# Reordered loads, norms and transposes in the forward and backward pass of a linear-attention block

## The chip, the cores and the metric

The kernel runs on one core of a Trainium2 chip. The time is the device time of one execution in microseconds (us), and the median of several executions stands for a kernel. A core has five engines that run beside each other and each take their instructions strictly in the order in which the program lists them: TensorE (PE, matmuls and transposes by matmul; its weight loads are shown as PEld), VectorE (DVE), ScalarE (ACT), GpSimd (POOL) and SyncE (SP, which here does nothing but issue DMAs). Matmuls write into PSUM, a small memory of a few banks, from which DVE and ACT take the results away. DMA transfers are issued from SP's queue (SPq), or from POOL's, and run on 16 DMA engines that all queues share.

## The reference

The kernel computes one transformer block and its whole gradient. With S = 2048 rows, D = 640 columns, H = 32 heads of 20 columns and F = 1728:

```
phi  = lambda t: where(t > 0, t + 1, exp(t)) + 1e-6
xn   = layernorm(x);  q, k, v = split(xn @ wqkv)
kv   = sum over s of phi(k)^T v        (per head);   z = sum over s of phi(k)
o    = (phi(q) kv) / (phi(q) z + 1e-6)
h    = x + o @ wo
hn   = layernorm(h)
out  = h + (silu(hn @ w1) * (hn @ w3)) @ w2
```

The outputs are `out` and, for a given `grad_out`, the gradients of x, wqkv, wo, w1, w3 and w2. Inputs and outputs are bf16.

## The kernel before

Rows are handled in 16 tiles of 128. The whole order of the work is written out by hand: the program lists the instructions of all engines in one sequence, and each engine takes its own out of it. Nothing is planned by a scheduler. So moving a call in the Python text moves its instructions on the queues of their engines, and only there. Where a tile is ready too late, the engine that wants it stands, and so does everything behind on that engine. A hardware DMA also waits until the eighth one before it has landed, since eight semaphores are used in turn.

The first part (about 0 to 85 us) goes over the row tiles t = 0 to 15 in one loop. Each pass makes K of tile t: five matmuls per half of 320 columns (`p1_half`, line 268) of the turned, normalized x (`pqT`) by the K columns of wqkv, into a PSUM tile `big` that has two buffers. ScalarE takes exp and relu out of it (`phi`, lines 295 and 296, tiles mq and rq), and two DVE instructions, held back by one tile (`held`, lines 299 and 300), make phi(k) of them in `pk_all`. At t = 6, 7, 9 and 11 a Q tile is made in the same way (`q_tile`), in the same PSUM buffers. From t = 7 on, TensorE also works on M = phi(k)^T xn (`m_part`, line 430). kv and v are never formed: M is multiplied by the V columns of wqkv later (`kvT_block`).

Ahead of its use a tile is normalized: DVE makes mean and variance (`stat`), POOL takes the inverse root (`ln_rs`, line 155), and then either DVE normalizes (line 161 and following), or, for the tiles 10, 12 and 14, ScalarE (`norm_act`, line 166), for which POOL also makes the bias `nb` (line 170). From tile 8 on, `p1_norm` then issues the transposing DMA into `pqT` (line 251) on SP. Where in pass t these steps stand is written in the table `v_steps`: "N" and "S" stand before the pass's own exp and relu, in turn with the held DVE instructions (R); "A" stands after the exp and relu and ahead of the Q tile of the pass, "B" behind the Q tile, and "L" after that.

Three tables and lists put DMAs into the passes: `outs` (stores of xn and phi(k) to DRAM, for later), `trickle` (pieces of w1 and w3; `w13` is the list of their loads), and the calls behind the loop. SP issues one DMA after the other, each 0.5 to 3.6 us, and a DMA whose source is not ready holds up all that follow on SP.

After the loop, M is finished row block by row block (`m_end`, which also sends each block through a transposing DMA to `mT`), the four tiles r of normalized phi(q) are made (`r_head` is `r_row`, DVE's work, and then `r_T`, a transposing DMA from SP), and the weights `wo`, `w1`, `w3` and `w2T` come in.

From 76 us on, `f2_wT` makes five blocks of the product of kv and wo, each turned by a DMA from SP into `Wp` (line 709). `f2_half` multiplies the turned r by Wp (lines 655 and 657), adds x, and makes the second layer norm's statistics; `f2_hn` normalizes. `q_out` and `r_store` store phi(q) and r to DRAM from POOL's queue. Then follow the MLP, its backward pass, and the backward pass of the attention.

In the last, at 555 us, `q_parts` leaves five blocks qp (here the tile `tri`), each copied from PSUM by ScalarE and DVE (line 1222 and following) and turned by a DMA from SP into `QT` (line 1226). The list of calls `part(n)` steps through them, with loads of the turned xn between (`load_xnT`, line 1242, each a single transposing DMA of 640 KB). After that come the squares for the gradients of kv and wo (lines 1369, 1388), while `fill(n)` puts half gradients of wqkv (line 1335) between them, and then the loads of phi(k) (`load_pk`, tile pkb), of M (`mN`, from `m_v`), the store of `dwoT_d` and the turned wq (`load_wqT`, line 1299).

The lines that order all this, next to those that the diff shows:

```
            for step in steps:
                if step is not R and step[0] == when:
                    p1_norm(step[1])
            if when == "A" and t in QT:
                q_tile(QT.index(t))
```

Of the kernel before, what the change touches and what calls it, by code (L numbers as in the profile page):

```python
# [9 lines left out]
P = 128  # L10
# [8 lines left out]
S, D, H, F = 2048, 640, 32, 1728  # L19
# [36 lines left out]
def kernel(  # L56
# [19 lines left out]
    V, A, T, G, SY = nc.vector, nc.scalar, nc.tensor, nc.gpsimd, nc.sync  # L76
    dma, dmaT, dmaG = SY.dma_start, SY.dma_start_transpose, G.dma_start

    def rows(ap):
        return ap.rearrange("(t p) d -> p t d", p=P)  # L80
# [50 lines left out]
    class Stats:  # L131
# [13 lines left out]
        def part(self, src, t, j, mid=None):  # L145
            if j == 0:
                self.st[t] = cp.tile([P, 2, 6], F32, name="st6", bufs=4)
            V.bn_stats(out=self.st[t][:, j, :], in_=src[:, t, j * HD:(j + 1) * HD])
            if j == 0:
                return  # L150
            V.bn_aggr(out=self.mv[:, t, :], in_=self.st.pop(t)[:])
            if mid is not None:
                mid()
            V.tensor_scalar(out=self.ve[:, t:t + 1], in0=self.mv[:, t, 1:2], scalar1=EPS_LN, scalar2=None, op0=ALU.add)
            G.tensor_tensor(out=self.rs[:, t:t + 1], in0=self.ve[:, t:t + 1], in1=mhalf[:, 0:1], op=ALU.pow)
# [27 lines left out]
    def load_wq(a, b):  # L183
        dma(out=wqkv[:, :, a * HD:b * HD], in_=wq_v[:, :, a * HD:b * HD])
# [62 lines left out]
    def p1_norm(t):  # L247
        xn = x_sb[:, t, :]
        (ln1.norm_act if on_act(t) else ln1.norm)(xn, xn, t)
        if t >= XT_DMA:  # L250
            dmaT(out=pqT[:, :, t * P:(t + 1) * P], in_=xn)
# [132 lines left out]
    def r_T(t):  # L384
        dmaT(out=pqT[:, :, t * P:(t + 1) * P], in_=pqs[t])
# [47 lines left out]
    def m_end(m, js=(0, 1)):  # L433
        mb = mbs[:, m % 4, :]
        acc = macc[m]
        for j in js:
            A.copy(out=mb[:, j * HD:(j + 1) * HD], in_=acc[j][:, 0:HD])
        if m < 2:
            A.copy(out=Z[:, m:m + 1], in_=acc[1][:, HD:HD + 1])
            z_diag(m)  # L440
        if m < DT - 1:
            dmaT(out=mT[:, :, m * P:(m + 1) * P], in_=mb)
# [13 lines left out]
    def load_w2T(a, b):  # L456
        dmaT(out=w2T[:, :, a:b], in_=B_w2[a:b, :])
# [45 lines left out]
    def load_wo():  # L503
        dma(out=wo[:], in_=A_wo.rearrange("(c p) n -> p c n", p=P))

    trickle = {4: w13[0], 5: lambda: w13[1](0, 1), 6: lambda: w13[1](1, 2), 12: w13[2]}

    R = None
    v_steps = {1: (R, ("N", 4)), 2: (("S", 5), R, ("N", 5)), 3: (("S", 6), R, ("N", 6), ("C", 0)),
               4: (("S", 7), R, ("N", 7), ("S", 8)), 5: (R, ("N", 8), ("S", 9)), 6: (R, ("N", 9), ("S", 10)),  # L510
               7: (("S", 11), R, R, ("A", 10), ("L", 11)), 8: (("S", 12), R, R, ("S", 13)),
               9: (("N", 13), R, ("S", 14), ("B", 12)), 10: (R, R, ("S", 15)), 11: (R, ("A", 14), ("L", 15))}
    V_OPS = {"S": stat, "N": p1_norm, "C": p1_scale}

    def xn_out(g, q):
# [12 lines left out]
    for t in range(ST):  # L528
        first = None
        if t < RAW:  # L530
            first = phi_tiles()
            kh = [ps.tile([P, 512], F32, name="k0", tag="m", bufs=2) for _ in range(2)]

            def act(i, j):
                A.activation(first[i][:, j * HD:(j + 1) * HD], kh[j][:, 0:HD], (AF.Exp, AF.Relu)[i],
                             scale=ln1.rs[:, t:t + 1])

            def between():
                act(0, 0)
                p1_tr(t + 1)  # L540
                act(1, 0)
            k = p1_mm(t, D, between, kh)
            act(0, 1)
            act(1, 1)
        else:
            k = p1_mm(t, D, (lambda: p1_tr(t + 1)) if t + 1 < XT_DMA else None)
        steps = v_steps.get(t, (R,) * len(held))
        for step in steps:
            if step is R:
                held.pop(0)()  # L550
            elif step[0] in V_OPS:
                V_OPS[step[0]](step[1])
        phi(k, pk_all[:, t, :], t, first)
        for when in ("A", "B", "L"):
# [5 lines that stand above are left out]
        if 3 <= t < 7:  # L560
            ghh_chunk(t - 3, lambda: ps.tile([P, 512], F32, name="gp", tag="m", bufs=2))
        m_part(0, M0.get(t, ()))
        if t >= 11:
            V.memset(bd[:, t - 11, :], 0.0)
            make_mask(t - 11)
        if t >= 9:
            m_part(1, [2 * (t - 9), 2 * (t - 9) + 1])
        for f, *n in outs.get(t, ()):
            f(*n)
        if t in trickle:  # L570
            trickle[t]()
# [5 lines left out]
    def r_row(t):  # L577
        r_red(t)
        r_inv(t)
        r_scale(t)  # L580

    def r_head(t):
        r_row(t)
        r_T(t)
# [4 lines left out]
    phi_rest()  # L589
    m_part(1, (14, 15))  # L590
    m_end(1)
    load_wq(4, 6)
    group_out(SC - 1)
    w13[3]()
    z_late((2, 3, 4), big())
    m_part(2, range(10))
    z_rows(((0, 1), (2, 3, 4)), ps.tile([P, 2, 512], F32, name="bigx", tag="big", bufs=2))
# [2 lines left out]
    r_prod(1)  # L600
    m_part(2, range(10, ST))
    m_end(2)
    load_wo()
    for go in w13[4:]:
        go()
    dmaG(out=m_v[:, 0, :], in_=mbs[:, 0, :])
    r_head(0)
    r_prod(2)
    phi_rest()
    m_part(3, range(5))  # L610
    q_tile(6)
    r_head(1)
    r_prod(3)
    phi_rest()
    m_part(3, range(5, 11))
# [4 lines left out]
    phi_rest()  # L620
    m_part(3, range(11, ST))
    m_end(3)
    r_T(2)
    load_w2T(4 * P, 8 * P)
    dmaG(out=m_v[:, 1:4, :], in_=mbs[:, 1:4, :])
    r_head(3)
    r_prod(5)
# [316 lines left out]
    def kv3():  # L944
# [3 lines left out]
    run((q_late, 10, f2_mT), (q_late, 11, kv3), (phi_rest,),  # L948
        (q_late, 12, lambda: (f2_wT(0), f2_wT(1))), (q_late, 13, lambda: (f2_wT(2), f2_wT(3))),
        (f2_wT, 4), (phi_rest,), (q_late, 14), (r_T, 4), (r_head, 5), (r_prod, 7),  # L950
        (q_out, 10, 14), (mlp_ghh, 4),
        (q_late, 15), (w2_room,), (sig_table,), (f2_half, 0, 0), (f2_half, 1, 0), (f2_half, 2, 0), (f2_half, 3, 0), (mlp_ghh, 5),
        (f2_half, 0, 1), (r_store, 4, 5), (f2_half, 1, 1), (f2_hn, 0), (r_store, 5, 6), (f2_half, 2, 1), (f2_hn, 1),
        (f2_half, 3, 1), (f2_m_out,),
        (f2_half, 4, 0, True), (mlp_ghh, 6), (f2_half, 4, 1, True), (f2_half, 5, 0, True), (r_red, 6, (0,)), (f2_hn, 2), (f2_hn, 3),
        (f2_ht, 2), (f2_ht, 3), (load_w2T, 8 * P, 10 * P), (mlp_ghh, 7), (r_red, 6, (1,)), (r_inv, 6), (r_scale, 6),
# [280 lines left out]
    def load_xnT(c):  # L1237

        if c % 2 == 0:
            both = ba.tile([P, 2, DT, W], BF16, name="xnT", tag="ggb", bufs=2)  # L1240
            xnT[c], xnT[c + 1] = both[:, 0], both[:, 1]
        dmaT(out=xnT[c], in_=xn_d[c * W:(c + 1) * W, :])
# [55 lines left out]
    def load_wqT(k):  # L1298
        dmaT(out=wqT[:, k * DT:(k + 1) * DT, :], in_=A_wqkv[:, k * D:(k + 1) * D])
# [12 lines left out]
    load_xnT(1)  # L1312
    part(4)
    part(4)
    load_xnT(2)
    part(20)
    V.reduce_sum(out=gz[:], in_=gz8[:], axis=AX.X)


# [58 lines left out]
        for _ in range(n):  # L1378
            next(jobs, None)

    load_xnT(3)
    load_wqT(0)
    fill(4)
    for m, (a, b) in enumerate(M_H):
        n = (b - a) * DH
# [14 lines left out]
    small = bv.tile([P, ST, D], BF16, name="small", tag="hnN")  # L1400
    mN, gkv_b, gm = (small[:, n:n + DT] for n in (0, DT, 2 * DT))
    gzd = small[:, 3 * DT, :].rearrange("p (m q) -> p m q", q=P)
    dma(out=mN, in_=m_v)
    dma(out=rows(dwoT_d), in_=dwoT[:])

    dx = pool("dx", "right")

    def load_pk(c):
        pkb[c] = dx.tile([P, 2, D], BF16, name="pkb", bufs=4)
        (dma if c < 4 else dmaG)(out=pkb[c][:], in_=pk_v[:, c * 2:(c + 1) * 2, :])  # L1410

    gzb = dx.tile([P, D], F32, name="gzb")
    g_k = gqkv[1] = U1.tile([P, ST, D], BF16, name="g_k", tag="S0")
    for n in range(4):
        load_pk(n)

    for i, (c, ms) in enumerate(SQ_BLOCKS):
        unload(square(wqT[:, 2 * DT:, :], gkvT, i), gm[:, i, :])
# [186 lines left out]
```

## Time and profile before

| | |
|---|---|
| time, median of 3 executions | 819.58 us (819.23 to 820.79) |
| the profiled execution's own time | 820.36 us |
| its span in the trace | 818.6 us (1.76 us lie outside the span) |
| TensorE's clock | 1.00 of full speed |
| TensorE (PE) busy | 811.6 us, 99% of the span |
| DVE, ACT, POOL busy | 55%, 40%, 16% |
| DMA | 162.46 MB, mean 198 GB/s |

How to read the lines that are shown further down. A line of an engine's timeline has the start in us, the duration in us, the engine, the line of the program, the operation, what it writes and reads, the shape, how many instructions were joined in it, and in brackets how long the engine had stood before it and whose end released it. SPq lines are DMAs as SP issues them: the duration is that of the issue, not of the transfer. Matmuls are pipelined and their ends are modelled, so the durations of neighbouring matmul lines overlap, and the start-to-start distance is what counts. The chain that ended last follows the work back from the last instruction, at each step to what released it.

### The profile page before, as it was taken

The numbers are of one execution on the slowest core, as the hardware profiler recorded it, in microseconds if no ns is written. First come the engines' busy times: TensorE is split into PE (matmuls) and PEld (weight loads), VectorE is DVE, ScalarE is ACT, GpSimd is POOL, SyncE is SP. The second block draws the span as 40 slices with busy tenths as digits, with TensorE's granted clock in tenths as the row PEclk, the third lists the DMA queues.
The fourth block names the chain that finished last, engine by engine and source line by source line (L and its number), as shares of the span: only waits on it lengthen the run. The fifth ranks groups of instructions, "written<-read, shape, count | busy, mean of one in ns | idle before, by whom it ended". The sixth has DMA issues, their size and how long they took to land.

```text
span 818.6 us, 13711 instructions
## 1 busy us (share of the span) xinstructions
PE 811.6 (99%) x5261; PEld 501.6 (61%) x5292; DVE 452.7 (55%) x973; ACT 324.8 (40%) x609; POOL 131.7 (16%) x198
## 2 busy tenths in 40 slices
PE   9999999999999999999999999999999999999998
PEld 6777544555555555754577777777777777544444
DVE  7859997998898566300057777772781544200000
ACT  7856688665565666011112212222212334211111
POOL 2243333323222212100001111110220000000000
PEclk9999999999999999999999999999999999999999
DMA  9899899696485556999877877269994888979991
GB/s 262 207 242 277 206 276 302 207 244 174 128 209 158 169 168 168 239 254 243 233 178 181 218 194 193 58 111 181 269 217 93 179 193 153 249 175 235 221 239 37
DMA packets 335889, 162.46 MB, mean 198 GB/s; under 512 B 252560, under 2 KB 329072, under 8 KB 335824
## 3 DMA queue, kind: packets, MB, share of 16 engines
q1 hardware_dynamic: 291920, 120.68, 63.8%
q0 software_dynamic: 7328, 24.48, 8.9%
q10 hardware_dynamic: 36576, 16.42, 8.2%
q8 instruction: 41, 0.67, 0.3%
q14 instruction: 24, 0.20, 0.1%
HBM read 47.09 MB, written 53.43 MB: 123 GB/s over the span
## 4 chain that ended last, share of the span: by engine, by line
PE 96%; DMA 1%; ACT 1%; DVE 1%; issue 0%; SPq 0%; POOL 0%; DVEq 0%
PE mm L395 20%; PE job L1335 19%; PE ghn L1131 14%; PE gxn L1504 8%; PE gw L1086 7%; PE big L268 4%; PE o L913 4%; PE o L859 3%; PE gwo L1219 3%; PE macc L430 3%; PE gr L1188 3%; PE dkv L1441 3%; PE at L657 2%; DMA wqkv<-in_A_wqkv_dram 1%; PE dkv L1369 1%; DMA tri<-tri 1%
## 5 line engine op out<-in xcount | busy, mean ns | idle before, releaser
L1335 PE MATMUL job<-gb,hnN 128*128 128x496 bf16 (+3 forms) x576 | 116.8, 366 | 0.0
L1131 PEld LDWEIGHTS <-ggb 128*128 128x128 bf16 x864 | 84.5, 98 | 33.0
L395 PE MATMUL mm<-pqT,w 128*128 128x512 bf16 x396 | 93.2, 379 | 0.5
L1335 PEld LDWEIGHTS <-hnN 128*128 128x128 bf16 x576 | 55.8, 98 | 61.0
L395 PEld LDWEIGHTS <-w 128*128 128x128 bf16 x540 | 52.6, 98 | 62.9 <-issue 0.6
L1339 ACT CAST obs<-job 128x496 bf16<-128x496 f32 (+4 forms) x56 | 28.5, 510 | 123.6 <-PE job L1335 123.6
L1131 PE MATMUL ghn<-w13a,ggb 128*128 128x320 bf16 x448 | 63.5, 299 | 0.0
L1146 DVE SCALAR_TENSOR_TENSOR wb<-gs,hnb 128x640 f32<-128x640 bf16 x16 | 13.2, 825 | 88.1 <-ACT gs L1143 88.1
L1131 PE MATMUL ghn<-w13b,ggb 128*128 128x320 bf16 x416 | 61.4, 299 | 0.0
L395 PE MATMUL mm<-g2T,w2T 128*128 128x512 bf16 x228 | 58.8, 379 | 0.6
L1086 PE MATMUL gw<-hb,g 128*128 128x512 bf16 (+2 forms) x316 | 58.4, 345 | 0.2
L1086 PEld LDWEIGHTS <-g 128*128 128x128 bf16 x320 | 31.3, 98 | 27.0
L420 ACT CAST ghh<-mm 128x512 bf16<-128x512 f32 x48 | 28.2, 588 | 48.2 <-PE mm L395 41.4
L1196 POOL TENSOR_TENSOR sz<-Zb,g_h 128x640 f32<-128x640 bf16 x16 | 20.2, 1262 | 163.7 <-DVE g_h L1197 163.7
L796 ACT ACTIVATE sig<-mm 128x512 bf16<-128x512 f32 x56 | 33.7, 602 | 25.0 <-PE mm L395 21.6
L1143 ACT ACTIVATE gs<-ghn 128x640 bf16<-128x640 f32 x16 | 11.3, 705 | 76.0 <-PE ghn L1131 76.0
L395 PEld LDWEIGHTS <-w2T 128*128 128x128 bf16 x260 | 25.4, 98 | 23.4
L268 PEld LDWEIGHTS <-pqT 128*128 128x128 bf16 x320 | 30.7, 98 | 13.5 <-ACT pqT L260 0.9
L268 PE MATMUL big<-wqkv,pqT 128*128 128x320 bf16 x250 | 38.4, 299 | 0.2
L1335 PEld LDWEIGHTS <-g 128*128 128x128 bf16 x320 | 31.0, 98 | 11.5
L832 DVE TENSOR_TENSOR gate<-gate,sig 128x1024 bf16<-128x1024 bf16 x28 | 19.3, 689 | 33.9 <-ACT gate L807 31.1
L1091 ACT CAST gw2o<-gw 128x512 bf16<-128x512 f32 (+2 forms) x20 | 10.4, 519 | 66.6 <-PE gw L1086 25.3
(217 smaller groups left out, 1391.2 us busy)
## 6 DMA issues: line engine op xcount, KB each, us to landing
hh_d<-hhT SPq DMA_DIRECT2D x24, 256.0 KB, 2.8
gg_d<-gate POOLq DMA_DIRECT2D x24, 256.0 KB, 4.4
gg_d<-ghh POOLq DMA_DIRECT2D x24, 256.0 KB, 4.1
ggb<-gg_d SPq DMA_DIRECT2D x6, 896.0 KB, 5.3
ggb<-gg_d ACTq DMA_DIRECT2D x6, 832.0 KB, 5.7
ggb<-gg_d SPq DMA_DIRECT2D x2, 1728.0 KB, 13.9
pk_d<-pk_all SPq DMA_DIRECT2D x4, 640.0 KB, 5.4
g<-in_grad_out_dram SPq DMA_DIRECT2D x4, 640.0 KB, 5.7
```

The lines of the kernel that those rows point to most:

```text
L268: T.matmul(acc, lhsT=pqT[:, c, t * P:(t + 1) * P], rhs=wqkv[:, c, n0:n0 + HD], start=(c == 0), stop=(c == DT - 1))
L395: T.matmul(acc[:], lhsT=w[:, c, fc * P:(fc + 1) * P], rhs=rhs[:, c, :], start=(c == 0), stop=(c == DT - 1))
L420: A.copy(out=ghh[n // 2][:, n % 2, :], in_=acc[:])
L430: T.matmul(macc[m][j][:, 0:n], lhsT=pk_all[:, t, m * P:(m + 1) * P], rhs=x_ext[:, t, j * HD:j * HD + n], start=(t == 0), stop=(t == ST - 1))
L796: A.activation(sig[:, i, :], gp[:], AF.Sigmoid)
L859: T.matmul(accs[i, j][:, 0:HD], lhsT=hhT[c][:, fc, i * P:(i + 1) * P], rhs=w2[:, fc, j * HD:(j + 1) * HD], start=(first and fc == 0), stop ...
L913: T.matmul(o2["ps"][:, 0:HD], lhsT=hhT[c][:, fc, i * P:(i + 1) * P], rhs=w2[:, fc, j * HD:(j + 1) * HD], start=(fc == 0), stop=(fc == FT - 1))
L1086: T.matmul(acc[:, 0:fw], lhsT=g2[:, t, m * P:(m + 1) * P], rhs=hb[b][:, t, 0:fw], start=(t == 0), stop=(t == ST - 1))
L1131: T.matmul(acc[:, j, 0:HD], lhsT=ggb[t // 2][:, k, lo:lo + P], rhs=rhs[:, j * HD:(j + 1) * HD], start=(k == 0), stop=(k == NG - 1))
L1335: T.matmul(acc[:, 0:n], lhsT=lhs[:, t, m * P:(m + 1) * P], rhs=rhs(t), start=(t == 0), stop=(t == ST - 1))
L1339: A.copy(out=ob, in_=acc[:, 0:n])
L1504: T.matmul(acc[:, j, 0:HD], lhsT=g, rhs=wqT[:, k, j * HD:(j + 1) * HD], start=(k == 0), stop=(k == 14))
```

## The change

The diff changes the order of calls only; the computation, the number of instructions and the tiles remain. TensorE's and DVE's instructions keep their order. In parts:

1. In the loop, the table `trickle` gets the second load of w1 at t = 7 (before: t = 12), the V columns of wqkv at t = 9 (before: after `m_end(1)`) and the second load of w3 at t = 13 (before: after the last `group_out`). `wo` and the rest of w1 and w3 are loaded after that last `group_out` (before: after `m_end(2)`), and w2T's columns 512 to 1023 after `m_end(2)` (before: after `r_T(2)`).
2. A new step "F" calls `p1_norm` ahead of the exp and relu of the pass. Tile 12's norm on ScalarE stands there at t = 9 (before: "B", behind the exp and relu of K tile 9 and Q tile 2), and tile 14's at t = 11 (before: "A", behind the exp and relu of K tile 11). The transposing DMA of tile 12 moves with it, ahead of that of tile 13.
3. `r_T(1)` goes from the row work of r tile 1 to after `m_end(3)`.
4. The two `r_store` calls of r tiles 4 and 5 stand before and after `q_out`, instead of among the first `f2_half` steps.
5. `load_xnT(2)` comes behind the last `part` step instead of ahead of it, so behind the last transposing DMA of tri.
6. The loads of pkb 0 and 1 come ahead of those of mN and the store of dwoT_d; `load_xnT(3)` and `load_wqT(0)`, which stood ahead of the squares, come behind the loads of pkb 2 and 3.

```diff
--- before.py
+++ after.py
@@ -503,13 +503,13 @@
     def load_wo():
         dma(out=wo[:], in_=A_wo.rearrange("(c p) n -> p c n", p=P))
 
-    trickle = {4: w13[0], 5: lambda: w13[1](0, 1), 6: lambda: w13[1](1, 2), 12: w13[2]}
+    trickle = {4: w13[0], 5: lambda: w13[1](0, 1), 6: lambda: w13[1](1, 2), 7: w13[2], 9: lambda: load_wq(4, 6), 13: w13[3]}
 
     R = None
     v_steps = {1: (R, ("N", 4)), 2: (("S", 5), R, ("N", 5)), 3: (("S", 6), R, ("N", 6), ("C", 0)),
                4: (("S", 7), R, ("N", 7), ("S", 8)), 5: (R, ("N", 8), ("S", 9)), 6: (R, ("N", 9), ("S", 10)),
                7: (("S", 11), R, R, ("A", 10), ("L", 11)), 8: (("S", 12), R, R, ("S", 13)),
-               9: (("N", 13), R, ("S", 14), ("B", 12)), 10: (R, R, ("S", 15)), 11: (R, ("A", 14), ("L", 15))}
+               9: (("F", 12), ("N", 13), R, ("S", 14)), 10: (R, R, ("S", 15)), 11: (("F", 14), R, ("L", 15))}
     V_OPS = {"S": stat, "N": p1_norm, "C": p1_scale}
 
     def xn_out(g, q):
@@ -548,6 +548,8 @@
         for step in steps:
             if step is R:
                 held.pop(0)()
+            elif step[0] == "F":
+                p1_norm(step[1])
             elif step[0] in V_OPS:
                 V_OPS[step[0]](step[1])
         phi(k, pk_all[:, t, :], t, first)
@@ -589,9 +591,10 @@
     phi_rest()
     m_part(1, (14, 15))
     m_end(1)
-    load_wq(4, 6)
     group_out(SC - 1)
-    w13[3]()
+    load_wo()
+    for go in w13[4:]:
+        go()
     z_late((2, 3, 4), big())
     m_part(2, range(10))
     z_rows(((0, 1), (2, 3, 4)), ps.tile([P, 2, 512], F32, name="bigx", tag="big", bufs=2))
@@ -600,16 +603,14 @@
     r_prod(1)
     m_part(2, range(10, ST))
     m_end(2)
-    load_wo()
-    for go in w13[4:]:
-        go()
+    load_w2T(4 * P, 8 * P)
     dmaG(out=m_v[:, 0, :], in_=mbs[:, 0, :])
     r_head(0)
     r_prod(2)
     phi_rest()
     m_part(3, range(5))
     q_tile(6)
-    r_head(1)
+    r_row(1)
     r_prod(3)
     phi_rest()
     m_part(3, range(5, 11))
@@ -620,8 +621,8 @@
     phi_rest()
     m_part(3, range(11, ST))
     m_end(3)
+    r_T(1)
     r_T(2)
-    load_w2T(4 * P, 8 * P)
     dmaG(out=m_v[:, 1:4, :], in_=mbs[:, 1:4, :])
     r_head(3)
     r_prod(5)
@@ -948,9 +949,9 @@
     run((q_late, 10, f2_mT), (q_late, 11, kv3), (phi_rest,),
         (q_late, 12, lambda: (f2_wT(0), f2_wT(1))), (q_late, 13, lambda: (f2_wT(2), f2_wT(3))),
         (f2_wT, 4), (phi_rest,), (q_late, 14), (r_T, 4), (r_head, 5), (r_prod, 7),
-        (q_out, 10, 14), (mlp_ghh, 4),
+        (r_store, 4, 5), (q_out, 10, 14), (r_store, 5, 6), (mlp_ghh, 4),
         (q_late, 15), (w2_room,), (sig_table,), (f2_half, 0, 0), (f2_half, 1, 0), (f2_half, 2, 0), (f2_half, 3, 0), (mlp_ghh, 5),
-        (f2_half, 0, 1), (r_store, 4, 5), (f2_half, 1, 1), (f2_hn, 0), (r_store, 5, 6), (f2_half, 2, 1), (f2_hn, 1),
+        (f2_half, 0, 1), (f2_half, 1, 1), (f2_hn, 0), (f2_half, 2, 1), (f2_hn, 1),
         (f2_half, 3, 1), (f2_m_out,),
         (f2_half, 4, 0, True), (mlp_ghh, 6), (f2_half, 4, 1, True), (f2_half, 5, 0, True), (r_red, 6, (0,)), (f2_hn, 2), (f2_hn, 3),
         (f2_ht, 2), (f2_ht, 3), (load_w2T, 8 * P, 10 * P), (mlp_ghh, 7), (r_red, 6, (1,)), (r_inv, 6), (r_scale, 6),
@@ -1312,8 +1313,8 @@
     load_xnT(1)
     part(4)
     part(4)
+    part(20)
     load_xnT(2)
-    part(20)
     V.reduce_sum(out=gz[:], in_=gz8[:], axis=AX.X)
 
 
@@ -1378,8 +1379,6 @@
         for _ in range(n):
             next(jobs, None)
 
-    load_xnT(3)
-    load_wqT(0)
     fill(4)
     for m, (a, b) in enumerate(M_H):
         n = (b - a) * DH
@@ -1400,9 +1399,6 @@
     small = bv.tile([P, ST, D], BF16, name="small", tag="hnN")
     mN, gkv_b, gm = (small[:, n:n + DT] for n in (0, DT, 2 * DT))
     gzd = small[:, 3 * DT, :].rearrange("p (m q) -> p m q", q=P)
-    dma(out=mN, in_=m_v)
-    dma(out=rows(dwoT_d), in_=dwoT[:])
-
     dx = pool("dx", "right")
 
     def load_pk(c):
@@ -1411,8 +1407,14 @@
 
     gzb = dx.tile([P, D], F32, name="gzb")
     g_k = gqkv[1] = U1.tile([P, ST, D], BF16, name="g_k", tag="S0")
-    for n in range(4):
-        load_pk(n)
+    load_pk(0)
+    load_pk(1)
+    dma(out=mN, in_=m_v)
+    dma(out=rows(dwoT_d), in_=dwoT[:])
+    load_pk(2)
+    load_pk(3)
+    load_xnT(3)
+    load_wqT(0)
 
     for i, (c, ms) in enumerate(SQ_BLOCKS):
         unload(square(wqT[:, 2 * DT:, :], gkvT, i), gm[:, i, :])
```

## The prediction

> **What bounds the kernel now.** I read the page's shares first, then the chain that ended last, then TensorE's timeline in each stretch that the diff touches, and last the queues feeding it there. The page (part 1, part 2's clock row, part 4):
>
> ```profile
> span 818.6 us, 13711 instructions
> PE 811.6 (99%) x5261; PEld 501.6 (61%) x5292; DVE 452.7 (55%) x973; ACT 324.8 (40%) x609; POOL 131.7 (16%) x198
> ...
> PEclk9999999999999999999999999999999999999999
> ...
> PE 96%; DMA 1%; ACT 1%; DVE 1%; issue 0%; SPq 0%; POOL 0%; DVEq 0%
> ```
>
> TensorE (PE) is busy for 99% of the span, at full clock, and 96% of the last chain is its own work. The diff removes no matmul, so it can only win places where TensorE waits, and lose by making new ones. Both are found on TensorE's timeline, where a gap stands in brackets:
>
> ```profile
> 39.98 1.52 PE L268 MATMUL big<-wqkv,pqT 128*128 128x320 bf16 x10
> ...
> 44.33 1.52 PE L268 MATMUL big<-wqkv,pqT 128*128 128x320 bf16 x10
> ...
> 85.57 2.88 PE L657 MATMUL at<-Wp,pqT 128*128 128x320 bf16 x20 [0.24 <-DVE rden L378]
> ...
> 566.50 0.78 PE L1388 MATMUL gkvT<-tri,woT 128*128 128x140 bf16 x10 [0.47 <-DMA tri<-tri]
> ```
>
> Between 24 and 85 us no line has a bracket: in the stretch where most of the diff lies, nothing is there to win. The two gaps shown are the only ones that the diff can close. Ends of matmuls are modelled, so I take start to start: consecutive 128x320 matmuls follow at 0.136 us, and by that measure the first gap costs 0.40 us and the second 0.63. A third, 0.25 us at 96.13 (the turned hn(3), late on DVE), keeps its cause. The measurement can't tell changes under about 0.2% (1.64 us) from none; so even both gaps together (1.03 us) lie below that.
>
> **ScalarE's norms, ahead of exp.** ScalarE (ACT) takes its instructions in order. Its timeline and POOL's:
>
> ```profile
> 32.40 0.70 ACT L295 ACTIVATE mq<-big 128x640 bf16<-128x640 f32 x1 [0.76 <-DVE pk_all L300]
> 33.00 0.70 ACT L296 ACTIVATE rq<-big 128x640 bf16<-128x640 f32 x1
> ...
> 34.84 0.92 ACT L166 ACTIVATE x_sb<-x_sb,nb,ln_rs 128x640 bf16<-128x640 bf16 x1
> ...
> 38.49 0.70 ACT L295 ACTIVATE mq<-big 128x640 bf16<-128x640 f32 x1 [0.76 <-DVE pk_all L300]
> 39.09 0.70 ACT L296 ACTIVATE rq<-big 128x640 bf16<-128x640 f32 x1
> 39.67 0.92 ACT L166 ACTIVATE x_sb<-x_sb,nb,ln_rs 128x640 bf16<-128x640 bf16 x1
> ```
>
> ```profile
> 32.21 0.41 POOL L170 TENSOR_SCALAR nb<-ln_mv,ln_rs 128x1 f32<-128x1 f32 x1
> ...
> 38.30 0.46 POOL L170 TENSOR_SCALAR nb<-ln_mv,ln_rs 128x1 f32<-128x1 f32 x1
> ```
>
> The norm needs nb, and POOL has nb(12) at 32.62 and nb(14) at 38.76, both after the exp that it now precedes could have run (32.40, 38.49). So norm 12 runs from about 32.66, the exp of tile 9 follows 0.81 later (39.67 to 40.48 is the same pair) at 33.47, and its relu ends at 34.76 instead of 33.70. K tile 10's first matmul, 34.44 before, writes the PSUM buffer that this relu releases (two buffers, in the order k9, q2, k10). Before, it started 0.74 after the relu's end, so that it did not wait; a matmul that waits starts about 0.06 after its releaser (566.45 to 566.50 at the tri gap). It now starts near 34.82: +0.38. Likewise norm 14 from 38.80, exp of tile 11 at 39.61 instead of 38.49, relu's end 40.90 instead of 39.79, and K tile 12, due at 39.98 + 0.38 = 40.36, starts near 40.96: +0.60. Together **+0.98 us**. Behind the norms queue only these exps and relus and those of the Q tile after each; the DVE adds that follow have gaps. DVE from 57 to 80 us has none, but it starts from TensorE's Z sums, so it moves along and gives nothing back. Bounds: 0 (if the exps catch up) and 1.11 (if tile 12 keeps the 0.19 that lay between the relu's end and its start).
>
> What the move buys is pqT(12) earlier: it landed at 39.43 for a need at 39.98. TensorE did not wait there, so that is worth nothing.
>
> **Bulk loads.** The w1 load (864 KB) goes from t = 12 to t = 7, behind xn_d; the V columns of wqkv (800 KB) go from after the loop to t = 9; w3 (832 KB) to t = 13; wo and the rest to about 55 us. All are due much later (77 us and after), and no byte is added. Each issue costs SP 0.5 to 1.2 us (its timeline has 1.12 for the w1 load); SP has idle time at these places. The price is in what is queued behind: the turned pqT(12), then pqT(14). In the trace the stretch from 43.2 (pk_d, xn_d, w1, pk_d: 2784 KB) has all landed at 55.45, some 265 GB/s with a starting delay near 1 us. xn_d and w1 together (1540 kB, from 33.0) are then through at 38.8; a turned tile issued behind a w3 part landed 0.7 after it (pqT(9)) and one 2.2 after it (pqT(10)); so pqT(12) lands at 39.5 to 41.0 against a need of 40.4 to 40.96. pk_d and V (1475 kB from 37.9) are through at 43.5, and pqT(14) lands at 44.2 to 45.7 against a need of 44.33 + 0.98 = 45.3. I take **0**, since three quarters of both spans lie ahead of the need; the bound above is 0.4 from these rows and 2 from lower rates (below). A gain is excluded, as no wait is here. At 52 to 75 us the turned mT(2) is issued earlier than before (it landed at 66.50 for 68.34), so nothing is late there.
>
> **The turned Wp blocks, 85 us.** SP's timeline:
>
> ```profile
> 77.38 1.40 SPq L187 DMA_DIRECT2D x_sb<-in_A_x_dram  x1
> 79.66 6.59 SPq L709 DMA_TRANSPOSE Wp<-pkx  x5
> ```
>
> The 0.24 gap is put down to DVE's rden, which was long done; the trace has Wp block 2 issued at 82.39 to 83.60 and landed at 85.48, and the matmuls start at 85.57. x_sb's 960 KB land at 83.44, among the blocks. Since r_T(1) and w2T now precede, SP is free sooner and the x_sb load goes at the end of its release, about 0.8 earlier. Blocks 3 and 4, behind no other load, landed 1.45 and 1.39 after their issue ended; block 2 would land at about 85.0 against 85.17. So **-0.40**; bounds -0.40 and 0 (if the issue time of 1.3 us a block is what counts). w2T's 512 columns, moved ahead of the turned r tiles on SP, and r_T(1), two places later, are needed from 82.7 and 85.6; their cover is over 10 us each.
>
> **tri and xnT(2), 560 us.** SP's timeline:
>
> ```profile
> 554.86 3.87 SPq L1226 DMA_TRANSPOSE tri<-tri  x3
> 558.77 3.34 SPq L1242 DMA_TRANSPOSE xnT<-xn_d  x1
> 562.21 1.22 SPq L1226 DMA_TRANSPOSE tri<-tri  x1
> ```
>
> The last tri block's copy by ACT ended at 561.5, but its transpose waited behind xnT(2)'s issue until 562.21 and landed at 566.45. With xnT(2) behind it, it issues from 561.5 and, with the 2.7 us median to landing, lands near 564.2, ahead of 565.86, when TensorE wants it; even the 4.25 us that it took here would do. **-0.63**, bounds -0.63 and 0 (d, below). Next late are the dkv buffers, with about 0.04 us to spare, so no more than that is taken away again. xnT(2) then lands near 568 (due about 596). xnT(3) and wqT(0), moved behind pk and dwoT_d, land near 580 and 584 (due 604 and 625); mN and dwoT_d may make SP idle for 3 us, as they wait for dwoT's squares; the pkT transposes end about 4 us later, with 5 us to spare. Cost 0; if that cover is gone, up to 1.
>
> **r_store.** Two POOL issues of 0.58 us move ahead of the ln_rs of rows 1 to 3. ve reaches POOL for those before DVE wants them: **0**; bound +0.5, the 96.13 gap growing by one issue.
>
> **Sum.** +0.98 + 0 - 0.40 - 0.63 + 0 = -0.05 us on the profiled execution's 820.36 (818.6 of span and 1.76 outside), 820.31. That execution is 0.78 above the median of the runs shown (819.58); taking it off, **819.5 us**: no difference.
>
> **Rivals.**
> (a) The norms ahead cost nothing: the 0.74 us of room absorbs it, as it would if nb came earlier. Then -1.03, 818.55. For it: nb(12) is only 0.2 later than the old exp; against: 0.81 + 0.2 exceed 0.74, and tile 12 had only 0.19. Still under 0.2%.
> (b) The other side: the bulk loads hold up the turned x tiles. It replaces the 0.98, as a late pqT covers ScalarE's delay. At the 209 GB/s that the window from 24 to 60 us has as its mean, 1475 kB from 37.9 are through at 45.0 and pqT(14) lands 1.4 later, 46.4: +2.07 against 44.33, net +1.0, 820.6. It decides when pqT(14) lands after 47.0 (2.67 late, to cover the 1.03 and 1.64), which takes a rate under 192 GB/s; with 165 it lands at 48.2, net +2.9, 822.5. For it: pqT(10), behind a w3 part, took 4.2 us, and the DMA row is at 9 tenths here. Against: most of that share is transposes, and xn_d and pk_d there landed 655 kB in 3.5 us, starting delay included.
> (c) Wp stays late: +0.35, 819.9, for SP's issue of 1.3 us a block.
> (d) tri lands no earlier, since xnT(1) and POOL's stores are in flight: 820.1.
>
> On (b): the Trainium skill, "DMA: Bandwidth & Descriptors", section "Queues, rings and completion order", says that each DMA engine consumes descriptors in the order of the ring, which for one issuing engine is one ring. By that rule a small transpose does not pass a bulk load of the same queue, and the place chosen for the loads can only cost. The trace agrees as far as it goes: pk_d, issued 1.2 us behind the w1 load, landed 1.66 behind it. By the rule alone, without a rate, the time is that of (b).
>
> **How the numbers follow.** Forecast (sum, with (c) and (d) as its variants) 0.50, (a) 0.17, (b) 0.28, of it two thirds past its point of decision or joined by another loss, something unforeseen 0.05. Slower by over 0.2%: 0.2 from (b), 0.04 from the unforeseen and 0.02 from the forecast's upper bounds, 0.26. Faster: only if more is to be won than the gaps on the timeline, 0.09. Within: 0.65. The range goes from 818.2, (a) with the r rows' gap as well, to 822.0, short of (b) at 165 GB/s.
>
> **What would show it.** In the changed kernel: brackets at K tiles 10 and 12 of 0.3 to 0.6 us, released by ACT's rq; no bracket at the L1388 and L657 groups; pqT(14) landed by 45.3. The prediction is wrong if a bracket with a pqT landing stands at 40 or 45 us, if gaps come at 580 to 625 us (xnT, pkT), or if the time leaves 819.6 by more than 1.64 us.

## The result, and the profile after

The changed kernel took 821.43 us (median of 10 executions) against 819.55 us for the kernel before (10 executions): a ratio of 1.0025, 95% interval 1.0015 to 1.0034. The medians lie 1.88 us apart, and the interval leaves out "no difference". The forecast was 819.5 us, no difference. The time itself lies inside the stated range of 818.2 to 822.0; that the kernel became slower does not fit the forecast.

The page of the changed kernel's profiled execution (821.89 us; span, busy shares, chain that ended last):

```profile
span 820.2 us, 13745 instructions
PE 812.9 (99%) x5292; PEld 501.2 (61%) x5292; DVE 452.7 (55%) x973; ACT 325.4 (40%) x609; POOL 131.4 (16%) x198
...
PE 93%; DVE 3%; DMA 2%; SPq 1%; issue 0%; ACT 0%; POOL 0%; DVEq 0%; ACTq 0%
```

The busy shares hardly differ from before (the 31 matmuls more are records that the first trace of before lacks; the second has 5292 too). The chain tells more: TensorE's part fell from 96% to 93%, and DVE, DMA and SP's queue came in. TensorE's timeline of the changed kernel has new brackets at four places (idle us, then who ended it):

```profile
35.11 1.52 PE L268 MATMUL big<-wqkv,pqT 128*128 128x320 bf16 x10 [0.61 <-ACT rq L296]
...
41.20 1.52 PE L268 MATMUL big<-wqkv,pqT 128*128 128x320 bf16 x10 [0.22 <-ACT rq L296]
...
45.98 1.53 PE L268 MATMUL big<-wqkv,pqT 128*128 128x320 bf16 x10 [0.26 <-DMA pqT<-x_sb]
...
94.90 0.85 PE L658 MATMUL at<-Wp,pqT 128*128 128x320 bf16 x5 [0.86 <-DMA pqT<-pql]
```

The first two are K tiles 10 and 12, waiting for ScalarE's relu; the third is K tile 14, waiting for its turned x; the fourth is the turned r tile 4. The brackets at 85 and 566 us are gone, as forecast. But the kernel before, profiled once more (819.31 us), has neither of them, with nothing changed. TensorE's timeline of that second profile:

```profile
85.11 2.88 PE L657 MATMUL at<-Wp,pqT 128*128 128x320 bf16 x20
...
564.46 1.73 PE L1388 MATMUL gkvT<-tri,woT 128*128 128x140 bf16 x25
```

The 25 gkvT matmuls now run as one group, where the first profile had 15, a wait, and 10. So I use this second profile as the base below. Both traces hold 5292 weight loads, in the same order. The difference of the starts of the same weight load in two traces, followed along the run, is a ladder: it rises by a step where one execution loses time. Against the second profile of before, the changed kernel's ladder is:

| where | step, us |
|---|---|
| the first 10 us | +0.13 |
| K tile 10, ScalarE's relu | +0.77 |
| K tile 12, ScalarE's relu | +0.38 |
| K tile 14, turned x | +0.43 |
| r tile 4, turned r | +1.03 |
| hn(3) and the MLP's first matmuls, net | -0.14 |
| everything after 100 us | 0.0 |
| sum (820.17 - 817.57) | +2.60 |

So 1.58 us come from the K loop, about 0.9 from r tile 4 and what follows it, and nothing from the parts behind 100 us. The medians differ by less than 2.60, since the second profile of before lies 0.24 below that kernel's median and the changed kernel's profile 0.46 above its own.

### The profile page after: what moved, and what is told of

Read it like the earlier page. It is cut to its first block, busy times and chain, and to the rows that moved or that the text cites. A ratio compares the mean times of both kernels' runs of the same rounds, so it can differ in the third digit from the quotient of the medians.

```text
span 820.2 us, 13745 instructions
## 1 busy us (share of the span) xinstructions
PE 812.9 (99%) x5292; PEld 501.2 (61%) x5292; DVE 452.7 (55%) x973; ACT 325.4 (40%) x609; POOL 131.4 (16%) x198
## 4 chain that ended last, share of the span: by engine, by line
PE 93%; DVE 3%; DMA 2%; SPq 1%; issue 0%; ACT 0%; POOL 0%; DVEq 0%; ACTq 0%
PE mm L395 20%; PE job L1336 20%; PE ghn L1132 14%; PE gxn L1506 8%; PE gw L1087 7%; PE o L914 4%; PE o L860 3%; PE gwo L1220 3%; PE gr L1189 3%; PE dkv L1443 3%; PE at L658 2%; PE macc L430 2%; PE big L268 1%; PE mm L268 1%; DVE st L148 1%; DMA pqT<-pql 1%
```

## The experiments

Times are ratios to the kernel before in the same session; their intervals are about +-0.1% (0.8 us), so single steps are read from the ladder, which is one execution of each kernel. Most kernels below are the kernel before with one part of the diff ("alone"), or the changed kernel with one part undone. The new places of w2T's columns and of `r_T(1)` were not run alone.

**Each part alone.** The norms:

```diff
-               9: (("N", 13), R, ("S", 14), ("B", 12)), 10: (R, R, ("S", 15)), 11: (R, ("A", 14), ("L", 15))}
+               9: (("F", 12), ("N", 13), R, ("S", 14)), 10: (R, R, ("S", 15)), 11: (("F", 14), R, ("L", 15))}
...
+            elif step[0] == "F":
+                p1_norm(step[1])
```

> The kernel before with only the norms of tiles 12 and 14 ahead of exp. Theory (each edit pays its own step of the difference of the two traces): K tile 10 waits about 0.8 us and K tile 12 about 0.4 us for ScalarE's relu, +1.15 us, about 820.7 against 819.55. Rival (ScalarE is late only because SP's transfers around it are late): no gap at these tiles, 819.5.

Measured 1.0015 (1.0006 to 1.0024). The ladder has +0.60 at K tile 10 and +0.30 at K tile 12, together 0.89, with all bulk loads in their old places. TensorE's timeline of this kernel:

```profile
34.85 1.52 PE L268 MATMUL big<-wqkv,pqT 128*128 128x320 bf16 x10 [0.43 <-ACT rq L296]
```

So the norms cost by themselves, for the reason that the prediction gave. ScalarE's timeline of the changed kernel shows it:

```profile
32.96 0.92 ACT L166 ACTIVATE x_sb<-x_sb,nb,ln_rs 128x640 bf16<-128x640 bf16 x1 [1.01 <-POOL nb L170]
33.79 0.68 ACT L295 ACTIVATE mq<-big 128x640 bf16<-128x640 f32 x1
34.37 0.69 ACT L296 ACTIVATE rq<-big 128x640 bf16<-128x640 f32 x1
...
39.05 0.92 ACT L166 ACTIVATE x_sb<-x_sb,nb,ln_rs 128x640 bf16<-128x640 bf16 x1 [0.69 <-POOL nb L170]
```

ScalarE stands 1.01 and 0.69 us for POOL's nb, with the exp of a finished K tile behind it in its queue. The relu ends at 35.06, and the waiting matmuls start at 35.11. The rival, no gap without the bulk loads, falls.

The bulk loads (w1, V and w3 into the loop, wo and the rest of w1 and w3 up from after `m_end(2)`):

```diff
-    trickle = {4: w13[0], 5: lambda: w13[1](0, 1), 6: lambda: w13[1](1, 2), 12: w13[2]}
+    trickle = {4: w13[0], 5: lambda: w13[1](0, 1), 6: lambda: w13[1](1, 2), 7: w13[2], 9: lambda: load_wq(4, 6), 13: w13[3]}
...
-    load_wq(4, 6)
     group_out(SC - 1)
-    w13[3]()
+    load_wo()
+    for go in w13[4:]:
+        go()
...
-    load_wo()
-    for go in w13[4:]:
-        go()
```

> The kernel before with only the bulk loads moved (w1, V columns and w3 into the loop, wo and the rest to after the last group_out). Theory (steps add up): only tile 14's turned x is late, by about 0.4 us, 820.0. Rival (bulk loads hold up whatever is turned behind them, and the norms ahead of exp cover a part of that): tile 12, now issued at 36.8 behind xn_d and w1, lands near 41.5 for a need at 40.0, tile 14 near 46.4 for 44.4; +1.9 us, 821.4.

Measured 1.0025 (1.0015 to 1.0035). Tile 12 landed at 39.96 and cost 0.1 at most; tile 14 landed at 45.84 and cost a step of 1.5 us on TensorE's timeline:

```profile
45.88 1.53 PE L268 MATMUL big<-wqkv,pqT 128*128 128x320 bf16 x10 [1.33 <-DMA pqT<-x_sb]
```

The rival had it right: the loads cost 1.5 us alone, not the 0.4 that they add to the norms. Its detail for tile 12 (41.5) was a miss here.

The r stores:

```diff
-        (q_out, 10, 14), (mlp_ghh, 4),
+        (r_store, 4, 5), (q_out, 10, 14), (r_store, 5, 6), (mlp_ghh, 4),
...
-        (f2_half, 0, 1), (r_store, 4, 5), (f2_half, 1, 1), (f2_hn, 0), (r_store, 5, 6), (f2_half, 2, 1), (f2_hn, 1),
+        (f2_half, 0, 1), (f2_half, 1, 1), (f2_hn, 0), (f2_half, 2, 1), (f2_hn, 1),
```

> The kernel before with only the r stores of tiles 4 and 5 around q_out. Theory: POOL's first r store waits for r tile 4 and pushes the 640 KB store of q into the time of the turned r tile 4, which lands over 3 us later: gap of about 1 us at r tile 4, the 0.25 us gap at hn(3) smaller, +0.8 us, 820.4. Rival (the gap at r tile 4 comes from TensorE and Wp being shifted, not from the stores): 819.5, no gap there.

Measured 1.0013 (1.0004 to 1.0022). The gap appears at r tile 4 although nothing ahead of the stores was moved and TensorE did not wait for Wp; the ladder has +1.18 there and +1.13 in all. TensorE's timeline:

```profile
93.40 0.85 PE L657 MATMUL at<-Wp,pqT 128*128 128x320 bf16 x5 [1.00 <-DMA pqT<-pql]
```

The last tri block's transpose ahead of xnT(2), with the transfers behind it (parts 5 and 6 of the diff):

```diff
+    part(20)
     load_xnT(2)
-    part(20)
...
-    load_xnT(3)
-    load_wqT(0)
     fill(4)
...
-    dma(out=mN, in_=m_v)
-    dma(out=rows(dwoT_d), in_=dwoT[:])
...
-    for n in range(4):
-        load_pk(n)
+    load_pk(0)
+    load_pk(1)
+    dma(out=mN, in_=m_v)
+    dma(out=rows(dwoT_d), in_=dwoT[:])
+    load_pk(2)
+    load_pk(3)
+    load_xnT(3)
+    load_wqT(0)
```

> The kernel before with only xnT(2) behind the last turned tri block and the pk, mN and dwoT_d transfers ahead of xnT(3) and wqT(0). Theory: the 0.63 us gap at 566 us goes and nothing comes in its place, 818.9. Rival (the later xnT(3), wqT(0) and pkT transfers give it back, or the time at 566 us is won again by waits behind it): 819.5 or more, with gaps between 575 and 630 us.

Measured 0.9998 (0.9990 to 1.0007): no difference. No gap at 566 us, none between 575 and 630, and also no gain, which the theory had put at 0.63. The gap was not in the usual execution of before. With the old order of these transfers, nine other executions were profiled (the second one of before and eight of kernels with this part untouched); a step at this place is in one of them, of 0.5 us. The theory's mechanism, SP's issue of xnT(2) ahead of the last block, is only a part of it. In the second profile SP was through with xnT(2) at 560.59 and issued the last block at 561.03, when its copies were done, so the order cost nothing. In the two executions with the gap (the first profile of before and the one just named) the block was issued 0.5 to 0.7 us late behind xnT(2), and it also landed 3.0 us after the end of its issue, where the second profile has 1.4. What made that transfer slow stays open.

**One part undone.** The changed kernel with the first diff of these, the norms, reversed:

> The changed kernel with the norms of tiles 12 and 14 back in their old places. Theory (tile 14's turned x lands near 45.9 behind the V columns whatever ScalarE does, so the larger of the two waits counts, not their sum): no gap at K tiles 10 and 12, one of 1.3 to 1.6 us at tile 14; about 821.4, no difference from the changed kernel's 821.43. Rival (steps add up): 1.15 less, 820.3.

Measured 1.0024 (1.0012 to 1.0037), as the changed kernel. Its TensorE timeline has the waits at other tiles, for the DMA now:

```profile
42.15 1.53 PE L268 MATMUL big<-wqkv,pqT 128*128 128x320 bf16 x10 [0.84 <-DMA pqT<-x_sb]
...
47.88 1.53 PE L268 MATMUL big<-wqkv,pqT 128*128 128x320 bf16 x10 [1.20 <-DMA pqT<-x_sb]
```

Steps of 1.0 at tile 12 and 1.4 at tile 14, and no wait for relu at tile 10 (this execution had lost 1.0 us before the first moved load was issued). So undoing the norms wins nothing: they cost about 1.1 us for ScalarE, and they bring tile 12's transpose forward, which the loads ahead of it would otherwise make late. It was expected that tile 12 has no gap; that was a miss.

The r stores' diff reversed:

> The changed kernel with the r stores of tiles 4 and 5 back in their old places. Theory: the gap of 1 us at r tile 4 goes, about 1.0 less, 820.4. Rival (the freed turned Wp blocks bring TensorE there before its operand anyway): 821.4 with a gap at r tile 4.

Measured 1.0017 (1.0003 to 1.0031). The gap at r tile 4 is gone, the ladder is +0.77, +0.38, +0.29 at tiles 10, 12 and 14, with 0.18 at tile 9 ahead of them, and ends at 1.60, 1.0 below the changed kernel's. The ratio agrees within its interval, and could not have told it alone.

V's load back behind the loop:

```diff
-    trickle = {4: w13[0], 5: lambda: w13[1](0, 1), 6: lambda: w13[1](1, 2), 7: w13[2], 9: lambda: load_wq(4, 6), 13: w13[3]}
+    trickle = {4: w13[0], 5: lambda: w13[1](0, 1), 6: lambda: w13[1](1, 2), 7: w13[2], 13: w13[3]}
...
     m_end(1)
+    load_wq(4, 6)
     group_out(SC - 1)
```

> The changed kernel with the V columns' load back behind the loop; w1 stays at t = 7 and the norms stay ahead of exp. Theory (V is the load that holds up tile 14): tile 14 lands near 43.5 and does not wait, the gaps at tiles 10 and 12 (about 1.1 us together) stay, about 0.4 less, 821.0. Rival (the w1 load ahead of it is enough): the gap at tile 14 stays, 821.4.

Measured 1.0011 (1.0000 to 1.0022). Tile 14 landed at 43.23 and did not wait, as expected. But a wait came at another place, for the turned third block of M:

```profile
70.10 0.48 PE L449 MATMUL bigx<-mT,wqkv 128*128 128x140 bf16 x5 [0.62 <-DMA mT<-hx]
```

V's 800 KB and then wo, w1 and w3 now all stand on SP ahead of mT(2), which landed at 70.05 (66.04 in the second profile of before) for a need near 69.2. Here r tile 4 had no gap, with the r stores as in the changed kernel: SP issued its transpose at 87.71, just ahead of the q store's 88.00, and it landed at 92.17, ahead of that store (92.85).

All three back at once (the last diff, and those of the norms and the r stores reversed):

> The changed kernel without the three parts that cost: V's load, the two norms and the two r stores back in their old places; the other moves stay. Theory (the 0.40 us gap at 85 us and the 0.63 us gap at 566 us of the first profile are not in most executions): 819.4, no difference from before. Rival (both are there as a rule, and these moves take them away): 818.5.

Measured 1.0027 (1.0003 to 1.0051), neither of the two expected results. TensorE's timeline shows what was left in:

```profile
40.62 1.53 PE L268 MATMUL big<-wqkv,pqT 128*128 128x320 bf16 x10 [0.59 <-DMA pqT<-x_sb]
69.55 0.48 PE L449 MATMUL bigx<-mT,wqkv 128*128 128x140 bf16 x5 [0.39 <-DMA mT<-hx]
...
609.57 1.52 PE L1444 MATMUL dkv<-small,xnT 128*128 128x320 bf16 x10 [0.55 <-DVE gp L1447]
...
628.27 0.85 PE L1507 MATMUL gxn<-wqT,bd 128*128 128x320 bf16 x5 [1.29 <-DMA bd<-g_k]
```

The w1 load at t = 7, without the norms ahead, makes tile 12 late (0.76 on the ladder); V, wo, w1 and w3, issued from 55 us on ahead of mT(2), make it late (0.57). The last two lie in the stretch that the prediction named for gaps at xnT and pkT, but wait for other transfers. At 610 us DVE had stood 0.92 us for a load of phi(k) that landed at 607.67. At 628 us it is the turned block bd, which SP issued at 624.39, after the pkT transposes that kept it busy until 621.85. Neither the changed kernel's profile nor the tri part's own has these waits. Of the seven profiles with xnT(2) behind the last tri block, two have a wait between 580 and 630 us (the other is the last kernel of this section); of the ten with the old order none has.

**The cost of one load, by place and by queue.** V alone to t = 9, in the kernel before:

```diff
-    trickle = {4: w13[0], 5: lambda: w13[1](0, 1), 6: lambda: w13[1](1, 2), 12: w13[2]}
+    trickle = {4: w13[0], 5: lambda: w13[1](0, 1), 6: lambda: w13[1](1, 2), 12: w13[2], 9: lambda: load_wq(4, 6)}
...
     m_end(1)
-    load_wq(4, 6)
```

> The kernel before with only the V columns' load moved, to t = 9 on SP. Theory (this load alone holds up tile 14): its turned x lands near 45.8, gap near 1.5 us at K tile 14, 821.2. Rival (it takes the w1 load at t = 7 too): landed by 44.4, no gap, 819.6.

Measured 1.0021 (1.0011 to 1.0030). V landed at 44.59 and tile 14's x at 45.31, a step of 1.09 us: most of the 1.5 of all the loads. The same from POOL's queue:

```diff
-    def load_wq(a, b):
+    def load_wq(a, b, q=dma):
-        dma(out=wqkv[:, :, a * HD:b * HD], in_=wq_v[:, :, a * HD:b * HD])
+        q(out=wqkv[:, :, a * HD:b * HD], in_=wq_v[:, :, a * HD:b * HD])
...
-    trickle = {4: w13[0], 5: lambda: w13[1](0, 1), 6: lambda: w13[1](1, 2), 12: w13[2], 9: lambda: load_wq(4, 6)}
+    trickle = {4: w13[0], 5: lambda: w13[1](0, 1), 6: lambda: w13[1](1, 2), 12: w13[2], 9: lambda: load_wq(4, 6, dmaG)}
```

> The same single move, but the V columns are loaded from POOL's queue. Theory of the queue's order (the turned tile waits because it stands behind the load on SP's queue): it lands by 44.4, no gap, 819.6. Theory of the shared engines (the load's bytes take the DMA engines' time from whichever queue): lands near 45.8 again, gap of over 1 us, 821.2.

Measured 1.0035 (1.0022 to 1.0048). POOL issued the load at 41.08, SP the transpose at 43.00, so nothing bulky was ahead of it on its own queue but the pk store of both kernels. V landed at 47.83 and the turned x at 48.48 (45.4 and 46.1 without the 2.4 us that this execution had lost before). So a place behind the load on SP's queue is not needed for the delay; the load's bytes on the shared DMA engines do it from POOL's queue too. The trace's single packets show it: V's run from 43.75 to 47.43, and SP's queue starts none between 43.69 and 46.83, although the issue of the transpose had ended at 44.20. TensorE's timelines, V from SP and then from POOL:

```profile
45.35 1.53 PE L268 MATMUL big<-wqkv,pqT 128*128 128x320 bf16 x10 [0.91 <-DMA pqT<-x_sb]
```

```profile
20.68 0.45 PE L258 MATMUL tr<-ident,x_sb 128*128 128x128 bf16 x5 [1.30 <-DVE x_sb L161]
...
48.53 1.53 PE L268 MATMUL big<-wqkv,pqT 128*128 128x320 bf16 x10 [1.68 <-DMA pqT<-x_sb]
```

(The wait at 20.68 stands before any changed instruction and belongs to this execution, not to the change: an x load landed at 18.09, against 15.39 in the second profile of before. The step at tile 14 is 1.85 against 1.09 from SP, since V, issued at the same point of the loop, landed 0.8 us later; why was not tried.) In both, the turned tile landed 0.7 behind the load. The Trainium skill, "DMA: Bandwidth & Descriptors", section "Issuing engines are not separate DMA queues", says that DMAs of all issuing engines run on the same 16 DMA engines and that another issuing engine saves issue time only; this run agrees. The order on SP's own queue, by which the prediction argued, is too narrow to explain it.

V behind tile 15's transpose, at the end of t = 11:

```diff
-    trickle = {4: w13[0], 5: lambda: w13[1](0, 1), 6: lambda: w13[1](1, 2), 12: w13[2], 9: lambda: load_wq(4, 6)}
+    trickle = {4: w13[0], 5: lambda: w13[1](0, 1), 6: lambda: w13[1](1, 2), 12: w13[2], 11: lambda: load_wq(4, 6)}
```

> The kernel before with only the V columns' load moved, to the end of pass t = 11, behind tile 15's turned x instead of ahead of tile 14's. Theory (it is the place ahead of tile 14 that costs, not the load inside the loop): no gap at K tiles 12 to 15, 819.5. Rival (the load's bytes cost wherever they lie in the loop): the gap moves to the next landing, the store's or mT's readers at 52 to 69 us, 820.5 or more.

Measured 1.0000 (0.9991 to 1.0009), with no step at K tiles 12 to 15. It is the place that costs. The profiled execution has the wait for Wp at 85 us, which is in others too (below).

w1 alone to t = 7, in the kernel before:

```diff
-    trickle = {4: w13[0], 5: lambda: w13[1](0, 1), 6: lambda: w13[1](1, 2), 12: w13[2]}
+    trickle = {4: w13[0], 5: lambda: w13[1](0, 1), 6: lambda: w13[1](1, 2), 7: w13[2]}
```

> The kernel before with only the w1 load moved, to t = 7. Theory (a turned tile waits for whatever was issued ahead of it): tile 12, issued at 36.8 behind it, lands 0 to 0.8 late, tile 14 in time; 819.5 to 820.3. Rival (w1 has 4 us less queued ahead of it there and is through by 38.2): no gap at all, 819.5.

Measured 1.0012 (1.0000 to 1.0025). Tile 12 landed at 40.72, a step of 0.55; tile 14 in time. The step is within the theory's 0 to 0.8; the median, 820.56, is a little above its 820.3.

**The q store first,** then both r stores:

```diff
-        (r_store, 4, 5), (q_out, 10, 14), (r_store, 5, 6), (mlp_ghh, 4),
+        (q_out, 10, 14), (r_store, 4, 6), (mlp_ghh, 4),
```

> The kernel before with the r stores of tiles 4 and 5 directly behind the q store, not around it. Theory (the first r store waits for r tile 4 on POOL and pushes the q store's 640 KB into the turned tile's time): the q store leaves at its old time near 85.6, the turned r tile 4 lands near 91 for a need at 92.5, no gap, 819.6. Rival (it is the r stores' own 320 KB beside it): gap of about 1 us at r tile 4 as with the stores around it, 820.8.

Measured 1.0008 (0.9997 to 1.0019). The step at r tile 4 fell from 1.18 to 0.17; a net 0.5 came at the turned hn soon after. The q store landed at 91.96, the r stores at 93.14 and 93.94, the turned r tile 4 behind all three at 94.20. Without the 1.9 us that this execution had lost before, the q store landed at its old time (90.0; 90.10 in the second profile of before) and the turned tile at 92.3, 1.4 us later than there (90.85). With the stores around the q store (the r stores alone, above) it landed at 93.35, 2.4 us later than there on the ladder. TensorE wants it 1.2 us after 90.85, so the first lateness costs 0.2 and the second 1.2. Both theories hold a part: the r stores' bytes are 1.4 us of the lateness, the push of the q store 1.0. The push is not a wait for r tile 4, as the theory had it (see the r stores, below).

**The kernel before, profiled once more:**

> The kernel before, unchanged, profiled once more. Theory (the gaps of 0.40 us at 85 us and 0.63 us at 566 us are accidents of the first profiled execution, whose time lay 0.8 above the median): at least one of them is missing, span near 817.6. Rival (they belong to the kernel): both are there again at these sizes.

819.31 us, span 817.6, neither gap. Of the sum's -1.03 nothing is left against this execution.

**The best guess for a better version** has V's load at t = 11, as above, and of the tri part only the move of xnT(2) behind `part(20)`:

> The version left over as the best guess: V's load at the end of t = 11 and only xnT(2) moved behind the last turned tri block. Theory (neither gap of the first profile is there as a rule): 819.4, no difference from before. Rival (the tri gap is common enough to show): 819.0.

Measured 1.0008 (0.9997 to 1.0020): no difference, and no version here beats the kernel before. The profiled execution (822.62 us, against a median of 820.23) waits for Wp at 86.5 and 91.3, 2.15 us together, and at a place where the kernel before does not:

```profile
587.89 1.52 PE L1440 MATMUL dkv<-small,xnT 128*128 128x320 bf16 x10 [0.99 <-DVE gp L1443]
```

Ahead of this wait, DVE had stood 2.39 us for the first load of phi(k). That load now follows xnT(2), xnT(3) and wqT(0) on SP and landed at 586.00, 4.8 us later than in the second profile of before on the ladder. The diff takes this away by part 6, which brings two of these loads forward. So part 5 without part 6 has a price of its own, as far as one profile can show it.

## Why the prediction was wrong

**The sum's base.** The step "-0.40 - 0.63" failed first. Both gaps were measured rightly, in an execution whose time lay 0.78 above the median, and they are 1.03 of the 1.05 us between it and the second execution (819.31). Taking the gaps off the sum and then 0.78 more off for the median counted them twice: 820.36 - 1.03 is 819.33 already. Against that one the two terms are 0, and the prediction's own remaining terms give 820.3. The Wp part did do something: in the five profiles with w2T and r_T(1) in their new places no wait for Wp is seen, while of twelve with the old places six have it, from 0.1 to 2.2 us on the ladder. That it lowers the time of the usual execution was not shown. On the ladder against the second profile, the forecast is off by 1.03 for these gaps, 0.9 for the r stores, 0.43 for the loads and 0.17 for the norms.

**The norms, +0.98.** Right in mechanism and place, 1.15 on the ladder of the changed kernel and 0.89 alone. The forecast for K tile 10 was low (0.38 against 0.77 and 0.60), that for tile 12 high (0.60 against 0.38 and 0.30). The split rests on a misread start: 34.44 is where the chain's stretch of these matmuls begins, while TensorE's timeline of the first profile has the first of them earlier:

```profile
34.27 1.52 PE L268 MATMUL big<-wqkv,pqT 128*128 128x320 bf16 x10
```

From there the same working gives 0.55 and 0.43, and the sum stays 0.98. In the changed kernel the norm of tile 12 began at 32.96, not 32.66, which adds to its first step.

**The bulk loads, "I take 0".** This failed. The estimate for tile 14 was 44.2 to 45.7 for a need of 45.3; it landed at 45.93. What was late is visible a step earlier: V was put through at 43.5 and landed at 45.37. The DMA transfers issued in the changed kernel from 39 to 44 us (KB each, us from issue to landing), and in the second profile of before from 40 to 43 us:

```profile
wqkv<-in_A_wqkv_dram SPq DMA_DIRECT2D x1, 800.0 KB, 7.3
pk_d<-pk_all SPq DMA_DIRECT2D x1, 640.0 KB, 4.7
...
pqT<-x_sb SPq DMA_TRANSPOSE x2, 5.2
```

```profile
pqT<-x_sb SPq DMA_TRANSPOSE x2, 2.6
```

(The pk_d shown is the next store, issued at 43.26. The one ahead of V was issued at 37.40 and landed at 43.04.) The working started pk and V at 37.9 on idle DMA engines, at 265 GB/s. But w1 landed at 39.78 instead of 38.8, and the turned tiles 12 and 13 stood behind it, landing at 40.46 and 41.70, so V landed 1.9 us behind the working. Each group was costed as though the one ahead of it were through. The rate was not what failed. By the trace's packets, the 1440 KB of pk and V moved from 40.40 to 44.75 us, some 340 GB/s, but began 2.5 us later than the working had it. (The 265 is itself a little high: 2784 KB in 11.25 us, the starting delay of 1 us taken off, are 253.) The wait that came, 0.43, is the size that the term named as its bound from these rows; alone, with no late K tile ahead of it, it was 1.51.

**Rival (b)** had the mechanism, that a late pqT covers ScalarE's delay instead of adding to it: 0.89 and 1.51 alone, 1.58 together. It was priced to decide only if tile 14 landed after 47.0, to outweigh the 1.03 that was not there. Without that credit a landing at 46 was enough, with the r stores. The chance that it got was too small by that same error. It also made the outcome hang on a low rate (under 192 GB/s), and the turned tile was late at a higher one.

**The r stores, 0 with a bound of +0.5.** This failed, and the cost was at a place that the term did not name. The prediction asked whether POOL's ln_rs would be late. What counted was what is on the DMA engines ahead of the turned r tile 4. POOL's timeline of the second profile of before, of the changed kernel, and then SP's of the changed kernel:

```profile
85.56 0.81 POOL L728 DMA_DIRECT2D pq_d<-pkx  x1
```

```profile
85.80 1.53 POOL L367 TENSOR_TENSOR pr<-pql,Zb 128x320 f32<-128x320 bf16 x2 [9.56 <-DVE rden L374]
87.27 0.60 POOL L736 DMA_DIRECT2D r_d<-pql  x1
87.87 0.76 POOL L729 DMA_DIRECT2D pq_d<-pkx  x1
88.62 0.55 POOL L736 DMA_DIRECT2D r_d<-pql  x1
```

```profile
88.23 4.59 SPq L385 DMA_TRANSPOSE pqT<-pql  x2
```

The expectations of two runs said that the first r store waits for r tile 4. It does not: DVE had finished that tile at 76.92, and the store goes out right after POOL's products, at the very place of the q store before (85.56, and TensorE is 1.71 us behind here). It keeps the q store back by its own issue of 0.60 us, and the r stores' 320 KB come on top. In the first profile of before the q store left 1.07 us ahead of the turned r tile 4 (85.62 and 86.69) and landed at 90.27, the tile at 91.00. Now it leaves 0.36 ahead, with a 160 KB store in front of it; it landed at 93.65 and the tile at 94.86.

**tri and xnT(2) behind 566 us.** Nothing was late in the changed kernel between 570 and 640 us, but the cover was thinner than reckoned. The last pkT transpose landed at 621.33, on the ladder 7.5 us later than in the first profile of before and 12.2 later than in the second, not 4. So the 0 of this term came out partly by luck, and two other kernels (at 588, and at 610 and 628 us) show waits in this stretch.

## What to carry to other kernels

A gap in one profile is a gap of that execution: before it enters a sum, look at how far that execution lies above the median, and whether a second profile has it. A load that nobody waits for still has a price where a small transfer that somebody does wait for is issued within its time on the DMA engines, from whichever queue; so place it behind the last such transfer (V at t = 11 cost nothing, at t = 9 it cost 1.1 us). When two changes delay the same consumer through different engines, the larger wait counts here, not the sum (0.89 and 1.51 us alone, 1.58 together), and undoing one of them wins little. A store that waits for nothing still pushes what is queued behind it, by its issue and by its bytes.

## What the runs showed of the hardware

- A turned 160 KB tile landed 0.6 to 0.7 us after the 800 KB load ahead of it, whether that load came from SP (44.59, 45.31) or from POOL (47.83, 48.48). Without it, the same transposes took 2.6 us from issue to landing.
- While an 800 KB load from POOL's queue moved (43.75 to 47.43), SP's queue started no packet from 43.69 to 46.83, with a transpose issued on it by 44.20.
- With nothing changed, executions of the kernel before went from 819.2 to 823.6 us. The profiles of the kernels here show steps at unchanged transfers that sometimes land late: an x load ahead of 18.7 us (in three profiles, of 0.7 to 1.5 us), the Wp blocks at 85 us (six of twelve with the old order), the last tri block at 566 us (two of ten).
